# Gate and up projections as seven-product 2x2 blocks with paused PSUM groups, and a steady stage laid out by time

## The chip, the cores and the metric

The kernel runs on one core of one Trainium2 chip. The metric is device time in microseconds, the median of several runs. The engines are TensorE (PE, matmuls; PEld are its weight loads), VectorE (DVE), ScalarE (ACT), GpSimd (POOL) and SyncE (SP, which here issues the DMAs). PSUM is the accumulator memory of TensorE, in banks of 128 x 512 FP32. Each engine works through its own instructions in the order in which the program lists them, and engines wait for each other by semaphores.

## The reference

Input x is [1, 2048, 576] in FP32. It is normalised; then an attention with 32 heads of 18 columns and a sliding window of 256 tokens is multiplied by the SiLU of a bilinear gated feed-forward layer with 4608 inner columns, and x is added.

```python
def _A_ref(x, wqkv, wo):
    H = 32; Dh = D // H; W = 256
    q, k, v = (x @ wqkv).reshape(B, S, 3, H, Dh) ...          # one per 576 columns
    scores = jnp.einsum("bhqd,bhkd->bhqk", q, k) * (Dh ** -0.5)
    mask = (idx[:, None] - idx[None, :] >= 0) & (idx[:, None] - idx[None, :] < W)
    p = _softmax(jnp.where(mask[None, None], scores, -1e9), axis=-1)
    return jnp.einsum("bhqk,bhkd->bhqd", p, v) ... @ wo

def _B_ref(x, w_gate, w_up, w_down):
    g = jnp.einsum("bsd,df->bsf", x, w_gate)
    u = jnp.einsum("bsd,df->bsf", x, w_up)
    return jnp.einsum("bsf,fd->bsd", g * u, w_down)

xn = _layernorm(x, axis=-1)
return x + _A_ref(xn, wqkv, wo) * _silu(_B_ref(xn, w_gate, w_up, w_down))
```

## The kernel before

Everything that TensorE multiplies is split into an FP16 high part and an FP16 low part, and a product is made as three passes (high x high, high x low, low x high). A product here means one matmul instruction: 128 contraction rows, 128 output rows, up to 512 columns, added up in a PSUM bank. With 576 = 4.5 x 128 contraction rows, a gate or up tile of 128 inner rows x 512 tokens takes 13 full products (`full_passes`, L896) and a half-height one of 64 rows (`half_pass`, L899 and L900, gate and up side by side as a pair).

*Prologue, to 184 us.* x is loaded, normalised and transposed into `XT` (high and low parts, tokens as columns); `XT2` holds the last 64 rows a second time, for the half products. V, Q and K are computed in two halves of 1024 tokens (`qk_tile`: L323 the products, L327 ACT's copy out, L328 DVE's low part) and stored to DRAM.

*Steady stage, 72 slots.* A slot is one of 18 groups of 256 inner rows and one of four chunks of 512 tokens. In a slot PE makes two gate tiles and two up tiles. ACT copies the gate tile out of PSUM (`gate_out`, L742, tile `gt`), DVE multiplies the up tile with it (`up_out`, L747, `ht`), and h is split (`h_hi` L752 on ACT, `h_lo` L757 on DVE). One slot later `down` makes 8 groups of six 288-column products (L770) in the single PSUM bank `dn`; DVE adds each to `acc` straight behind it (L775, the eviction).

One attention step (two heads, 512 queries) also runs in each of 64 slots. PE makes four scores at a time (L647); DVE adds the mask and takes the maximum (L655, `mx`); POOL makes of that the bias of the exponential (L657); ACT takes the exponential (L662, `sm_`) and casts it to the high part (L665, `pp`); the low part is a subtraction on DVE for one head and on POOL for the other (L670); SP issues the transpose by DMA (L673, `pt`); PE multiplies with V (L682, bank `pv`, `weigh`), and `finish` divides by the sum. Step s runs in slot s + 1.

The weights of the next group are prepared beside this. `ffn_raw` loads gate, up and down weights into `raw0`, `raw1`, `raw2`; `ffn_amax` (L356) takes maxima over their rows on DVE; `ffn_spread_out` joins them, two tiles in one (`am`), and writes them to DRAM (`sd_f`, L132); `ffn_spread_in` reads them back to all partitions (L136, `spread`); `ffn_scale` (L369 and the small operations L122 to L126) makes power-of-two scales `sc` of them on DVE; ACT (L147) and DVE (L150) split the weights with these, and POOL scales the high part of the down weights (L394).

*End, from about 1589 us.* The last down groups, then 16 `o_out`: the output projection (L860), SiLU, product, sum and store, with loads (`o_load`) four token tiles ahead.

*What sets the order.* Nothing reorders instructions. In the steady stage `at(slot, place, f, ...)` enters a step into one of 16 places of a slot, and the last loop walks through slots and places: at each place it lists 3 or 4 products, then the steps entered there, scores first and down groups next. That order is the order of every engine's queue and of SP's DMA issues.

```python
for n in range(8):
    at(sl + 1, (... (7, 9, 11, 13, 15, 17, 19, 21))[n], down, sl, n)
```

A place beyond 15 falls into the next slot.

Of the kernel before, what the change touches and what calls it, by code (L numbers as in the profile page):

```python
# [20 lines left out]
def kernel(  # L21
# [66 lines left out]
    def up_ring():  # L88
        return ring.tile([128, 10, 128], F16, name="upw", bufs=8)

    def dn_ring():
        return ring.tile([128, 3, D], F16, name="dnw", bufs=4)

    def h_ring():
        return ring.tile([128, 2, 512], F16, name="hh", bufs=4)

    def f_ring(name):
        return ring.tile([128, 512], F32, name=name, bufs=1)
# [8 lines left out]
    idle = const.tile([128, 512], BF, name="idle")  # L107
# [12 lines left out]
    def power(m, p, s):  # L120

        nc.vector.tensor_scalar(p, m, LEAST, MOST, op0=OP.max, op1=OP.min)  # L122
        pi = p.bitcast(mybir.dt.int32)
        nc.vector.tensor_scalar(pi, pi, 0x7F800000, None, op0=OP.bitwise_and)
        nc.vector.reciprocal(s, p)
        nc.vector.tensor_scalar(s, s, WTOP, None, op0=OP.mult)  # L126
# [38 lines left out]
    def full_passes(w, c):  # L165
        return passes(w, XT[:, :, c * 512:(c + 1) * 512])

    def half_pass(w, c, upper):

        r = slice(64, 128) if upper else slice(0, 64)  # L170
        return w[r, 9], (XT2[r] if upper else XT[r, 4])[:, c * 512:(c + 1) * 512]

# [5 lines left out]
    XN = {}  # L178
# [6 lines left out]
    XR = {}  # L185
# [9 lines left out]
    def stats(t):  # L195
# [8 lines left out]
        XN[t] = (sm, q)  # L204
# [15 lines left out]
    def parts(a, eng, src, h):  # L220
        eng.tensor_tensor(a[:, D:D + 64], src[:, 512:D], h[:, 512:D], op=OP.subtract)
        eng.tensor_tensor(a[:, D + 64:2 * D], src[:, 0:512], h[:, 0:512], op=OP.subtract)

    def norm1(t):
        xr, (sm, q) = XR.pop(t), XN[t]
        xn = XN[t] = pro.tile([128, D], F32, name="xn", bufs=3)
        nc.scalar.activation(xn, xr, AF.Identity, bias=sm[:, 3, q:q + 1], scale=sm[:, 1, q:q + 1])

    def norm2(t, whole=True):
# [21 lines left out]
    def turned(t, a=None, b=None):  # L251
# [6 lines left out]
        nc.scalar.copy(XT2[64:128, cs], b[64:128])  # L258
        nc.scalar.copy(XT[0:64, 4, cs], b[0:64])

    def turned_low(t, eng=nc.vector):
# [3 lines left out]
        eng.tensor_tensor(XT[64:128, 4, cs], b[64:128], XT2[64:128, cs], op=OP.subtract)  # L265
# [6 lines left out]
    rqk = pro.tile([128, 5, 2 * D], F32, name="rqk")  # L272
# [94 lines left out]
    def ffn_scale(g):  # L367
        sc = SC[g] = ring.tile([128, 12], F32, name="sc", bufs=3)
        nc.vector.tensor_reduce(sc[:, 0:3], SC.pop((g, "sp")), axis=AX.X, op=OP.max)  # L369
        power(sc[:, 0:3], sc[:, 3:6], sc[:, 6:9])  # L370
        nc.gpsimd.tensor_tensor(sc[:, 9:10], sc[:, 3:4], sc[:, 4:5], op=OP.mult)
        nc.gpsimd.tensor_scalar(sc[:, 9:10], sc[:, 9:10], C_FFN, None, op0=OP.mult)
        nc.gpsimd.tensor_tensor(sc[:, 9:10], sc[:, 9:10], sc[:, 5:6], op=OP.mult)

    def up_hi(g, k):
        w = UW[g, k] = up_ring()
        hi(w[:, 0:5], RAW[g, k % 2][:, :, k // 2 * 128:k // 2 * 128 + 128], SC[g][:, 6 + k % 2:7 + k % 2])

    def up_lo(g, k):
        w = UW[g, k]  # L380
# [140 lines left out]
    for t in range(16):  # L521
# [24 lines left out]
        if t % 8 < 7:  # L546
            continue
# [392 lines left out]
```

## Time and profile before

| what | us |
| --- | --- |
| median of 3 runs | 1653.02 (1652.64 to 1653.95) |
| span of the profiled execution | 1651.6 |
| prologue, to the first slot | 183.7 |
| one slot, first quarter of them / the others | 19.36 / 19.83 |
| steady stage ends, about | 1589 |
| PE busy | 1638.3 (99%) |
| DVE / ACT / POOL busy | 1185.1 / 913.6 / 596.2 |

The span is that of one profiled execution; its own time is not recorded beside it, so the runs' median stands 1.4 us above the span. A row of the page's groups reads: line, engine, operation, output tile <- input tiles, shape, count | busy time, mean ns of one | idle time of the engine before it and who ended it. A row of the chain or timeline reads: start, length, engine, line, operation. In a row of stretches stand length, then busy time and count for PE, PEld, DVE, ACT and POOL, the granted clock of PE, the share of DMA time and GB/s. SPq is SP's queue with its DMA issues.

### The profile page before, as it was taken

Reading aid. Unit: us, or ns where it says so; the run is one execution under the profiler, and the core shown is the slowest. Engines: PE = TensorE matmul, PEld = TensorE weight load, DVE = VectorE, ACT = ScalarE, POOL = GpSimd, SP = SyncE. Lnnn points to the kernel's source line nnn. Section 1 sums busy time; section 2 is a strip of 40 time slices with the busy share of each in tenths; the row PEclk is TensorE's granted clock in tenths of the full one; section 3 lists DMA queues with packets and bytes.
Section 4 is the critical chain, followed back from the end, with each engine's and each line's share of the span. In section 5 each row is a group of like instructions: output and inputs, shape, how many; then the busy total and the mean of one; then the engine's idle time right before and its main releaser. Section 6 shows DMA issues by size and latency. Waiting matters only on the chain.

```text
span 1651.6 us, 33875 instructions
## 1 busy us (share of the span) xinstructions
PE 1638.3 (99%) x12307; PEld 933.2 (56%) x12307; DVE 1185.1 (72%) x2985; ACT 913.6 (55%) x1578; POOL 596.2 (36%) x1043
## 2 busy tenths in 40 slices
PE   8999999999999999999999999999999999999999
PEld 5464455555555555555555555555555555555577
DVE  7533577777777878787878777878787787865544
ACT  6431465656565666676666666665666666632230
POOL 3110134445343535454444444444444443511000
PEclk9999999999999999999999999999999999999999
DMA  9482445455556766665666575757665656650228
GB/s 239 134 216 90 116 84 115 90 114 104 114 106 132 142 124 135 109 146 112 145 135 142 105 147 105 151 105 145 138 135 113 140 116 129 126 123 28 60 69 219
DMA packets 535079, 206.39 MB, mean 125 GB/s; under 512 B 473856, under 2 KB 513664, under 8 KB 534912
## 3 DMA queue, kind: packets, MB, share of 16 engines
q1 hardware_dynamic: 534912, 204.23, 57.8%
q8 instruction: 97, 1.59, 0.4%
q14 instruction: 70, 0.57, 0.1%
HBM read 76.63 MB, written 23.75 MB: 61 GB/s over the span
## 4 chain that ended last, share of the span: by engine, by line
PE 93%; DMA 3%; DVE 1%; SPq 1%; POOL 1%; issue 1%; ACT 0%; POOLq 0%; ACTq 0%
PE up L896 47%; PE dn L770 25%; PE up L323 5%; PE pv L682 4%; PE up L899 3%; PE s L647 2%; DMA pt<-pp 2%; PE s L860 2%; PE up L860 1%; PE s L291 1%; PE s L770 1%; PE up L291 1%; SPq L337 1%; DMA xr<-in_A_x_dram 0%; SPq L238 0%
## 5 line engine op out<-in xcount | busy, mean ns | idle before, releaser
L896 PE MATMUL up<-XT,upw 128*128 128x512 f16 x3744 | 926.8, 378 | 0.0
L770 PE MATMUL dn<-dnw,hh 128*128 128x288 f16 x3360 | 504.5, 286 | 0.0
L896 PEld LDWEIGHTS <-upw 128*128 128x128 f16 x3744 | 331.1, 97 | 279.6 <-issue 0.6
L775 DVE SCALAR_TENSOR_TENSOR acc<-dn,sc,acc 128x288 f32<-128x288 f32 x528 | 272.2, 516 | 285.9 <-PE dn L770 285.8
L770 PEld LDWEIGHTS <-hh 128*128 128x128 f16 x3456 | 326.1, 98 | 199.0 <-issue 41.1
L657 POOL TENSOR_SCALAR mx<-mx,sig 128x1 f32<-128x1 f32 x512 | 193.5, 378 | 551.3 <-DVE mx L655 526.2
L682 PEld LDWEIGHTS <-pt 128*128 128x128 f16 x2880 | 137.3, 96 | 62.9 <-DMA pt<-pp 5.2
L682 PE MATMUL pv<-vt,pt 128*128 128x37 f16 x2880 | 143.0, 179 | 2.9 <-DMA pt<-pp 2.9
L742 ACT ACTIVATE gt<-up 128x512 f32<-128x512 f32 x144 | 85.4, 593 | 84.5 <-PE up L899 81.4
L752 ACT ACTIVATE hh<-ht 128x512 f16<-128x512 f32 x144 | 89.9, 624 | 61.5 <-DVE ht L747 61.5
L747 DVE SCALAR_TENSOR_TENSOR ht<-up,gt 128x512 f32<-128x512 f32 x144 | 99.0, 688 | 16.6 <-PE up L896 6.6
L757 DVE SCALAR_TENSOR_TENSOR hh<-hh,ht 128x512 f16<-128x512 f16 x144 | 98.7, 685 | 0.0
L323 PE MATMUL up<-XT,upw 128*128 128x512 f16 x448 | 97.0, 379 | 0.0
L356 DVE TENSOR_REDUCE am<-raw 128x1 f32<-128x640 f32 (+1 forms) x108 | 85.0, 787 | 3.0 <-DMA raw<-in_B_w_gate_dram 3.0
L394 POOL TENSOR_SCALAR dnw<-dnw 128x576 f16<-128x576 f16 x36 | 69.1, 1921 | 23.0 <-ACT dnw L147 20.3
L147 ACT ACTIVATE upw<-raw,sc 128x640 f16<-128x640 f32 x72 | 59.2, 824 | 26.1 <-DVE sc L126 26.1
L323 PEld LDWEIGHTS <-upw 128*128 128x128 f16 x448 | 43.8, 98 | 52.5
L328 DVE SCALAR_TENSOR_TENSOR qp<-up,qp 128x512 f16<-128x512 f32 x36 | 24.7, 685 | 59.4 <-ACT qp L327 42.7
L150 DVE SCALAR_TENSOR_TENSOR upw<-raw,sc,upw 128x640 f16<-128x640 f32 x72 | 63.1, 876 | 0.1
L647 PE MATMUL s<-ks,qs 54*128 54x384 f16 (+2 forms) x512 | 60.2, 312 | 0.0
L327 ACT ACTIVATE qp<-up 128x512 f16<-128x512 f32 x36 | 21.4, 597 | 66.6 <-PE up L323 56.1
L899 PE MATMUL up<-XT,upw 64*128 64x512 f16 x144 | 55.7, 387 | 0.0
(2227 smaller groups left out, 2123.1 us busy)
## 6 DMA issues: line engine op xcount, KB each, us to landing
raw<-in_B_w_down_dram SPq DMA_DIRECT2D x36, 288.0 KB
raw<-in_B_w_gate_dram SPq DMA_DIRECT2D x36, 256.0 KB
raw<-in_B_w_up_dram SPq DMA_DIRECT2D x36, 256.0 KB
qk_d<-qp SPq DMA_DIRECT2D x112, 72.0 KB
vt<-v_d SPq DMA_DIRECT2D x48, 111.0 KB
ks<-qk_d SPq DMA_DIRECT2D x96, 54.0 KB
v_d<-vo SPq DMA_DIRECT2D x16, 296.0 KB
xr<-in_A_x_dram SPq DMA_DIRECT2D x16, 288.0 KB
```

What stands on the lines that cost most here:

```text
L323: nc.tensor.matmul(ps, a, b, start=i == 0, stop=i == len(pl) - 1)
L647: nc.tensor.matmul(ps[:, :hi_ - lo_], QS[s][r, i * 128:(i + 1) * 128], KS[s][r, lo_:hi_], start=True, stop=True)
L657: nc.gpsimd.tensor_scalar(mx[:, 1:2], mx[:, 0:1], sig[:, 1:2], shift, op0=OP.mult, op1=OP.add)
L682: nc.tensor.matmul(PVB[s][:, j, i, :VW], pt[:, 2 * nb * j + n], VT[s][:, lo_ + n % nb, j * VW:(j + 1) * VW], start=n == 0, stop=n == 2 * n ...
L742: nc.scalar.activation(g, ps, AF.Copy, scale=G_SC)
L747: nc.vector.scalar_tensor_tensor(h, ps, U_SC, GT.pop((sl, ft)), op0=OP.mult, op1=OP.mult)
L752: nc.scalar.activation(hh[:, 0], h, AF.Copy, scale=1.0 / LO)
L757: nc.vector.scalar_tensor_tensor(hh[:, 1], hh[:, 0], -LO, h, op0=OP.mult, op1=OP.add)
L770: nc.tensor.matmul(ps[:, :HALF], a, b, start=q == 0, stop=q == len(l) - 1)
L775: nc.vector.scalar_tensor_tensor(d, ps[:, :HALF], SC[g][:, 9:10], d, op0=OP.mult, op1=OP.add)
L896: nc.tensor.matmul(banks[up], a, b, start=i == 0 and not up, stop=i == 12 and up == 1)
L899: nc.tensor.matmul(banks[0], *half_pass(w, c, False), start=False, stop=True)
```

## The change

*Gate and up as blocks.* The unit of work becomes 128 gate rows and the same 128 up rows by 1024 tokens, taken as two sets of four 128-token tiles (even and odd). The contraction is cut into two halves of two 128-row blocks. The 2x2 block product is then formed from seven products P1 to P7 of sums of weights (`ws`, made on POOL by `ffn_sums` from `raw0` and the rescaled `raw1`) and sums of tokens (`TX`, made once from the transposed x by `t_form`; `t1` takes the place of x's odd tiles in `XT`). Each is six matmuls. The last 64 rows are made without blocks: `t11`, `t22` with two matmuls, `t21`, `t12` with one and a half-height one. A slot is group, tile k of the two, half q of the tokens, so there are 72 again.

*Paused groups.* Bank A collects P1, P6, P7, P4 and a tail; bank C collects P2, P5 and P3 with tails. Both are read in the middle of their accumulation: A by ACT after P1, P6 and P7 (`copy_out`), C by DVE after P2, P5 and P3 (`add_out`). `times_0` on DVE multiplies from A at the end, `times_1` on POOL multiplies what lies in SBUF.

*Order by time.* `at(slot, t, ...)` now takes a time within a slot of 18.65, `W` holds most of the times, and all steps are sorted by it. Down groups run three slots later and two groups behind that, so that 26 of them follow the last slot. Maxima, spread and scale stand closer to each other.

*Attention.* The score's operation on DVE multiplies by a scale and takes a minimum, a small ACT copy makes the bias, POOL's step L657 goes; exponentials stay single; the casts on ACT and the subtractions, now all on POOL, take both heads at once. Buffers of `pp` go from 3 to 2, of `pt` from 3 to 4. Scores are made in one slot ahead (0 and 1) and in the slot itself (2 and 3). Outputs of attention are stored every fourth step.

*Elsewhere.* `XT2` and its copies go. At the end `o_load` runs eight tiles ahead, into buffers of the weights.

```diff
+    def t_form(p, step):
+        q, m = divmod(p, 4)
+        cs = slice(2 * p * 128, (2 * p + 2) * 128)
+        t1 = t1s[:, m]
+        to = TX[:, q, :, :, m * 128:(m + 1) * 128]
+        if step == 0:
+            nc.gpsimd.tensor_tensor(x32p, XT[:, 0:4, cs], XT[:, 5:9, cs], op=OP.add)
+        elif step == 1:
...
+            for d, a, b in ((t1, o1, e1), (tf[:, 0], o2, t1), (tf[:, 1], o2, o1), (tf[:, 2], e2, tf[:, 0])):
+                nc.vector.tensor_tensor(d, a, b, op=OP.subtract)
+        elif step == 2:
+            nc.scalar.copy(to[:, :, 0:2], tf)
+            nc.vector.tensor_tensor(to[:, :, 2:4], tf, to[:, :, 0:2], op=OP.subtract)
...
+    def ffn_ratio(g, k):
+        r = RAW[g, 1][:, :, k * 128:(k + 1) * 128]
+        nc.gpsimd.tensor_scalar(r, r, SC[g][:, 10:11], 1.0 / WF, op0=OP.mult, op1=OP.mult)
+    def ffn_sums(g, k, part):
...
+            nc.gpsimd.tensor_tensor(s_[:, d:d + 2] if d < 8 else s_[:, 8], x_, y_, op=op)
...
-        nc.gpsimd.tensor_scalar(mx[:, 1:2], mx[:, 0:1], sig[:, 1:2], shift, op0=OP.mult, op1=OP.add)
...
-        nc.scalar.activation(sm, sm, AF.Exp, bias=mx[:, 1:2], scale=sig[:, 0:1])
...
+        nc.vector.tensor_tensor_reduce(sm[:, j, :n], ps[:, :n], bias[:, 384 - n:], sig[:, 1:2], 3e38,
+                                       op0=OP.add, op1=OP.min, accum_out=mx[:, j:j + 1])
+    def probs(s, i):
+        nc.scalar.activation(mx[:, 2:4], mx[:, 0:2], AF.Copy, bias=shift)
+        for j in range(2):
+            nc.scalar.activation(sm[:, j, :n], sm[:, j, :n], AF.Exp, bias=mx[:, 2 + j:3 + j], scale=-1.0)
+    def probs_hi(s, i):
+        nc.scalar.copy(pp_of(s, i)[:, :, 0], sm[:, :, :n])
...
-        (nc.gpsimd if j else nc.vector).tensor_tensor(pp[:, a + n:a + 2 * n], sm, pp[:, a:a + n], op=OP.subtract)
...
+        nc.gpsimd.tensor_tensor(pp[:, :, 1], sm[:, :, :n], pp[:, :, 0], op=OP.subtract)
...
-        todo.setdefault(slot * 16 + place, []).append((f, a))
+    T = 18.65
+    W = {"ttr": [0.18, 0.51, 3.42, 3.58, ...], ..., "amax": [13.45, 14.1, 14.89, 14.7, 17.23, 17.23], "scale": 7.11, ...}
+    def at(slot, t, f, *a):
+        todo.append((slot * T + t, len(todo), f, a))
...
+    PROD = {"P1": (0, 0, 5, "e1"), "P2": (0, 2, 5, "e2"), "P3": (2, 6, 9, "o2"), "P4": (1, 0, 3, "t4"),
+            "P5": (2, 0, 9, "t1"), "P6": (2, 2, 9, "t2"), "P7": (2, 4, 9, "t3")}
+    TAIL = {"t11": (0, 4, 5, 0), "t21": (1, 2, 3, 0), "t22": (1, 2, 3, 1), "t12": (2, 8, 9, 1)}
...
+    def copy_out(sl, name, bk):
+        FT[sl, name] = f_ring()
+        nc.scalar.activation(FT[sl, name], BK[bk], AF.Copy, scale=E_SC)
+    def add_out(sl, name, bk):
+        nc.vector.scalar_tensor_tensor(f, BK[bk], E_SC, f, op0=OP.mult, op1=OP.add)
+    def times_0(sl):
+        nc.vector.scalar_tensor_tensor(f, BK["A"], E_SC, f, op0=OP.mult, op1=OP.mult)
+    def times_1(sl):
+        nc.gpsimd.tensor_tensor(f, f, FT[sl, "a3"], op=OP.mult)
...
+            for kind, t in ((1, 0.0), (2, 0.3), (0, 11.5)):
...
+                    at(b - 3, t + 0.1 * part, ffn_raw, g, kind, part)
+            for n in range(6):
+                at(b - 3, W["amax"][n], ffn_amax, g, (1, 1, 2, 2, 0, 0)[n], n % 2)
+            at(b - 3, 18.2, ffn_spread_out, g)
+            at(b - 2, 2.0, ffn_spread_in, g)
+            at(b - 2, W["scale"], ffn_scale, g)
...
+    def down_at(sl, n, t):
+        u = 8 * (sl - 3) + n - LAG
+        if 0 <= u < NDOWN:
+            at(sl, t, down, u)
+            at(sl, t + 0.75, down_out, u)
+    for sl in range(NSLOT):
+        at(sl, 0.0, prod, sl, "A", "P1", 0, 6, True)
+        at(sl, 1.3, copy_out, sl, "a1", "A")
+        down_at(sl, 0, 1.29)
+        at(sl, 2.03, prod, sl, "C", "P2", 0, 4, True)
+        down_at(sl, 1, 2.9)
+        at(sl, 3.62, prod, sl, "C", "P2", 4, 6)
+        at(sl, 4.0, tail_, sl, "C", "t11")
+        at(sl, 4.49, add_out, sl, "a1", "C")
+        at(sl, 5.2, prod, sl, "A", "P6")
+        at(sl, 6.5, copy_out, sl, "a2", "A")
+        down_at(sl, 2, 6.5)
+        at(sl, 7.25, prod, sl, "C", "P5", 0, 4, True)
+        down_at(sl, 3, 8.5)
+        at(sl, 9.25, prod, sl, "A", "P7")
+        at(sl, 10.56, copy_out, sl, "a3", "A")
+        at(sl, 10.55, prod, sl, "C", "P5", 4, 6)
+        at(sl, 11.0, tail_, sl, "C", "t22")
+        at(sl, 11.45, add_out, sl, "a3", "C")
+        down_at(sl, 4, 11.4)
+        at(sl, 12.15, prod, sl, "A", "P4")
+        at(sl, 13.5, tail_, sl, "A", "t21", False)
+        down_at(sl, 5, 13.7)
+        at(sl, 14.45, prod, sl, "C", "P3", 0, 3)
+        down_at(sl, 6, 15.1)
+        at(sl, 15.85, prod, sl, "C", "P3", 3, 6)
+        at(sl, 16.5, tail_, sl, "C", "t12", False)
+        at(sl, 16.7, tail_half, sl, "A", "t21")
+        at(sl, 16.8, tail_half, sl, "C", "t12")
+        at(sl, 17.0, times_0, sl)
+        at(sl, 17.6, add_out, sl, "a2", "C")
+        down_at(sl, 7, 17.9)
...
```

DVE in the slot in which the maxima of a group are taken, after the change. L880 is `times_0`, L876 `add_out` (tiles `ft`), L372 the maxima, L377 their join, L920 the eviction of a down group:

```order
L880 SCALAR_TENSOR_TENSOR ft_9780<-up_9752,ft_9780 128x512
L372 TENSOR_REDUCE am_9964<-raw0_9944 128x1 x2
L876 SCALAR_TENSOR_TENSOR ft_9842<-up_9753,ft_9842 128x512
L377 TENSOR_TENSOR am_9964<-am_9964 128x3
L920 SCALAR_TENSOR_TENSOR acc_1962<-dn_10034,sc_7848,acc_1962 128x288
```

The maxima of the gate weights stand between the two last reads of PSUM in that slot, and the join ahead of the eviction of the eighth down group.

SP in the same place, after the change. L748 are the transposes of probabilities, L786 and L789 the stores of attention's output, L124 and L128 the way of the maxima out to DRAM and back:

```order
L748 DMA_TRANSPOSE pt_9962<-pp_9959 128x12x128
L786 DMA o_d1_84<-ob_9047 128x4x144
L789 DMA o_d1_84<-ob_9047 128x4x144
L124 DMA sd_f8_10042<-am_9964 128x3
L128 DMA spread_10072<-sd_f8_10042 128x384
L748 DMA_TRANSPOSE pt_10093<-pp_10086 128x12x128
```

SP before, in the corresponding place (L132 and L136 are the two ways, L673 the transposes, L634 the load of V):

```order
L132 DMA sd_f9_11759<-am_11318 128x3
L634 DMA vt_11775<-v_d_82 128x6x74
L673 DMA_TRANSPOSE pt_11820<-pp_11773 128x12x128
L711 DMA o_d1_84<-ob_7159 128x1152
L136 DMA spread_11849<-sd_f9_11759 128x384
L673 DMA_TRANSPOSE pt_11896<-pp_11823 128x12x128
```

The way out and the way back had three other transfers between them and now follow each other.

DVE in the slot after that, before the change (L369 and L122 to L126 are the scale, L775 evictions, L655 the scores):

```order
L670 TENSOR_TENSOR pp_11967<-sm__11927,pp_11967 128x384
L775 SCALAR_TENSOR_TENSOR acc_1888<-dn_11976,sc_10764,acc_1888 128x288
L369 TENSOR_REDUCE sc_11990<-spread_11849 128x3
L122 TENSOR_SCALAR sc_11990<-sc_11990 128x3
L124 TENSOR_SCALAR sc_11990<-sc_11990 128x3
L125 RECIPROCAL sc_11990<-sc_11990 128x3
L126 TENSOR_SCALAR sc_11990<-sc_11990 128x3
L775 SCALAR_TENSOR_TENSOR acc_1888<-dn_12024,sc_10764,acc_1888 128x288
```

And DVE there after the change (L892 is `h_lo`, L385 and L114 to L118 the scale):

```order
L876 SCALAR_TENSOR_TENSOR ft_10067<-up_10046,ft_10067 128x512
L892 SCALAR_TENSOR_TENSOR hh_10099<-hh_10099,ft_9842 128x512
L385 TENSOR_REDUCE sc_10146<-spread_10072 128x3
L114 TENSOR_SCALAR sc_10146<-sc_10146 128x3
L116 TENSOR_SCALAR sc_10146<-sc_10146 128x3
L117 RECIPROCAL sc_10146<-sc_10146 128x3
L118 TENSOR_SCALAR sc_10146<-sc_10146 128x3
L920 SCALAR_TENSOR_TENSOR acc_1962<-dn_10131,sc_7848,acc_1962 128x288
```

In both the scale stands between two evictions; it has stands in the slot right behind the one whose maxima it reads.

ACT in the slot in which most of a tile's weights are split, after the change (L139 are the high parts of weights, L872 `copy_out`, L729 the small copy, L731 exponentials, L736 the cast):

```order
L139 ACTIVATE wg_9256<-raw0_8795,sc_8997 128x640
L872 ACTIVATE ft_9266<-up_9179 128x512
L139 ACTIVATE wu_9340<-raw1_8599,sc_8997 128x384
L729 ACTIVATE mx_9289<-mx_9289 128x2
L731 ACTIVATE sm__9288<-sm__9288,mx_9289 128x384 x2
L139 ACTIVATE ws_9347<-sums_9126,sc_8997 128x512
L872 ACTIVATE ft_9351<-up_9179 128x512
```

Three splits of weights now stand around two copies out of PSUM bank A, where before the splits stood between exponentials and casts and one copy out per half slot.

523 lines of the change are left out of this document (299 added, 224 removed).

## The prediction

> **What bounds it now.** I read the page's engine shares and chain first, then who TensorE waits for, then a piece of the chain inside the steady stage, then the busy times of single slots.
>
> ```profile
> span 1651.6 us, 33875 instructions
> PE 1638.3 (99%) x12307; PEld 933.2 (56%) x12307; DVE 1185.1 (72%) x2985; ACT 913.6 (55%) x1578; POOL 596.2 (36%) x1043
> PE 93%; DMA 3%; DVE 1%; SPq 1%; POOL 1%; issue 1%; ACT 0%; POOLq 0%; ACTq 0%
> ...
> PE pv L682 <- DMA pt<-pp: 2.9, 5, 0.9
> ...
> 847.53 0.73 PE dn L770 x6
> 848.27 1.29 PE up L896 x6
> ...
> 850.30 0.14 PE pv L682 x6
> ...
> 851.46 0.65 PE up L896 x3
> ...
> 854.14 0.32 PE up L899
> 854.46 0.00 PE up L900
> 854.46 0.33 PE s L647 x4
> 854.79 0.84 PE dn L770 x6
> ...
> 923.56:943.40 19.84, 19.84 (x163) 11.25 (x163) 15.41 (x42) 11.77 (x20) 9.33 (x17) 1.00 0.52 111
> 943.40:963.20 19.80, 19.80 (x161) 11.22 (x160) 16.16 (x41) 14.46 (x26) 9.59 (x15) 1.00 0.63 117
> ```
>
> TensorE is busy for 99% and makes 93% of the chain; all its waits for other engines together are a few us. In the pieces of the chain (start, length, what) a 512-column product costs 1.29/6 = 0.215, a group of six down products 0.73 (0.84 just after scores), a pair of half-height products 0.32 (0.10 of it before the first starts), four scores 0.33, six PV products 0.14. The last two rows are one slot each: length, then busy time of PE, PEld, DVE, ACT, POOL. A slot takes 19.8 with no hole in PE at clock 1.00; DVE has about 4 us to spare, ACT 5 to 8, POOL 10. So time falls as fast as products are taken from PE, until a handoff to another engine shows.
>
> **What goes.** Before, a slot holds 4 x 13 = 52 full gate/up products and two half pairs. After: seven products of six, six full ones for the last 64 rows, and one half pair: 48 full and one pair. Per slot 4 x 0.215 = 0.86, and of a pair 0.22; its other 0.10 I leave in, since the scores at 7.02 then follow full-height products directly. 1.08 x 72 slots = **-77.8 us**. Added up by the same rows, the new slot lasts 18.7: P1 1.29, then down groups, products and attention in the order of the table, with the seventh down group ending at 18.7.
>
> **What is added beside it.** For the costs I take these rows.
>
> ```profile
> L775 DVE SCALAR_TENSOR_TENSOR acc<-dn,sc,acc 128x288 f32<-128x288 f32 x528 | 272.2, 516 | 285.9 <-PE dn L770 285.8
> L747 DVE SCALAR_TENSOR_TENSOR ht<-up,gt 128x512 f32<-128x512 f32 x144 | 99.0, 688 | 16.6 <-PE up L896 6.6 <-ACT pp L665 2.8 <-issue 0.9
> L742 ACT ACTIVATE gt<-up 128x512 f32<-128x512 f32 x144 | 85.4, 593 | 84.5 <-PE up L899 81.4 <-PE s L647 1.8
> L147 ACT ACTIVATE upw<-raw,sc 128x640 f16<-128x640 f32 x72 | 59.2, 824 | 26.1 <-DVE sc L126 26.1
> L356 DVE TENSOR_REDUCE am<-raw 128x1 f32<-128x640 f32 x72 | 58.2, 809 | 3.0 <-DMA raw<-in_B_w_gate_dram 3.0
> L208 ACT ACTIVATE sm<-mv,eps_t 128x2 f32<-128x2 f32 x8 | 2.4, 296 | 11.2 <-DVE mv L203 11.2
> ...
> 909.99 0.71 ACT L662 ACTIVATE sm__12853<-sm__12853,mx,sig 128x384 f32<-128x384 f32 x1 [0.29 <-POOL mx L657]
> 910.73 0.51 ACT L665 CAST pp<-sm__12853 128x384 f16<-128x384 f32 x1
> ...
> 910.03 0.91 POOL L670 TENSOR_TENSOR pp<-sm__12824,pp 128x384 f16<-128x384 f32 x1
> ...
> L670 POOL TENSOR_TENSOR pp<-sm__8300,pp x1: 1603/1603/1603, 620.0 to 620.0; 128x384 f16<-128x384 f32 x1
> ```
>
> DVE per slot: two more PSUM reads (2 x 0.69) and some 450 more weight columns (0.6), less four subtractions (of the size that takes POOL 0.91) that go to POOL: about even, 15 to 16 of 18.7. ACT: one more copy out (0.59), four small copies (4 x 0.30), 0.6 of weights, less what four wide casts save against eight: 13 to 15. POOL: four double subtractions of at most 2 x 0.92 (7.4), one product, sums and ratio, less eight bias steps: 12 to 14. No engine reaches 18.7, so what the edits cost is waits at single handoffs. Four of these I price.
>
> (a) *Down groups six and seven.* The single `dn` bank goes to DVE and back.
>
> ```profile
> 901.61 0.90 PE L770 MATMUL dn<-dnw,hh 128*128 128x288 f16 x6
> 902.54 0.52 DVE L775 SCALAR_TENSOR_TENSOR acc<-dn,sc,acc 128x288 f32<-128x288 f32 x1 [1.09 <-PE dn L770]
> ...
> 95.04 0.69 DVE L328 SCALAR_TENSOR_TENSOR qp<-up,qp 128x512 f16<-128x512 f32 x1 [5.39 <-DMA qk_d<-qp]
> 95.79 1.46 PE L323 MATMUL up<-XT,wq 128*128 128x512 f16 x6 [1.45 <-DVE qp L328]
> ```
>
> PE is free for its next product at 901.61 + 0.73 = 902.34, DVE starts 0.20 later and takes 0.52; PE starts 0.06 after DVE's end. A round trip is 0.78 even with DVE idle. Between `down_at(sl, 5, ...)` and `down_at(sl, 6, ...)` stand three products, 0.65: a wait of 0.13 in each of the 69 slots with down groups, **+9.0**. Every other gap has four products (0.86) or more. Behind the waiting group stands everything on PE, so it is paid in full.
>
> (b) *The maxima slot* (one of four). DVE holds, after the last products of bank A: `times_0` 0.69, two maxima 0.81 each, `add_out` 0.69, the join of the maxima 0.16, then the eviction 0.52. From 18.7 - 1.8 + 0.13 + 0.20 = 17.3 that ends at 21.0. The next slot's first down group wants the bank at 18.85 + 1.29 = 20.14. That would be 0.9; neighbours on DVE may overlap in part, which can bring it to nothing. I take the middle, 0.4 x 16 = **+7**, between 0 and 0.9 each.
>
> (c) *The scale chain.* The maxima go to DRAM and come back to all partitions before DVE's `ffn_scale`, which stands ahead of an eviction in DVE's order.
>
> ```profile
> 1474.74 0.33 SPq L132 DMA_DIRECT2D sd_f<-am  x1
> ...
> 1477.05 0.32 SPq L136 DMA_DIRECT2D spread<-sd_f  x1
> ...
> 1531.75 0.33 SPq L132 DMA_DIRECT2D sd_wo<-woa  x1
> 1539.24 0.33 SPq L136 DMA_DIRECT2D spread<-sd_wo  x1
> ...
> 921.04 0.83 SPq L132 DMA_DIRECT2D sd_f<-am  x1
> ...
> 926.38 0.53 SPq L136 DMA_DIRECT2D spread<-sd_f  x1
> ...
> 169.95 0.35 SPq L136 DMA_DIRECT2D spread<-sd_f  x1
> 173.80 0.67 DVE L369 TENSOR_REDUCE sc<-spread 128x3 f32<-128x384 f32 x1 [0.71 <-DMA spread<-sd_f]
> 175.12 0.17 DVE L126 TENSOR_SCALAR sc<-sc 128x3 f32<-128x3 f32 x1
> ```
>
> The way out takes 2.3 (1474.74 to 1477.05) up to 7.5 (the `wo` pair), in the steady stage at most 5.3 (921.04 to 926.38); the way back 3.85 (169.95 to 173.80); the scale itself 1.5. Before, these stood some 16 us apart. After, the maxima are joined at about 20.1 of their slot, the two transfers follow each other on SP, and `ffn_scale` is reached by DVE at about 5.9 of the next slot. I take 2.5 out, near the row that has an `o_d` store beside it as here: 20.2 + 2.5 + 0.1 + 3.85 = 26.65, or 7.8 of the next slot. Scale until 9.3, eviction and release until 9.9; PE wants the bank for its fourth down group at 8.5, with (b) at 8.9. Stall about 0.9 x 16 = **+14**; with 2.3 out 0.7, with 5.3 out 3.7. Queued behind it on DVE: two scores, `finish`; on POOL the ratio; on SP nothing, since the way out has landed by then.
>
> (d) *The weights slot* (one of four). On ACT, between the first and the third copy out, stand 0.59 + 3 small copies 0.9 + 6 exponentials 4.3 + two casts of at most 2 x 0.9 + one 0.62 + weights 0.82, 0.6 and 0.72 + two copies 1.2 = 11.5, from 1.5: it ends at 13.0, or 12 with overlaps, where the fourth product wants bank A at 12.1. 0.25 x 17 = **+4**, between 0 and 0.9.
>
> At the start, slots 0 to 2 have no down groups: 12.8 us of PE each, against about 13 of ACT and chains of score, exponential, subtraction and transpose (0.33 + 0.7 + 0.9 + 4 or more). I put **+5** there, between 0 and 12.
>
> **At nothing.** The token sums in the prologue and the end's loads:
>
> ```profile
> 101.00:184.00 83.00, 83.00 (x483) 47.12 (x482) 27.43 (x49) 21.65 (x42) 3.49 (x8) 1.00 0.44 129
> 1596.00:1648.00 52.00, 51.95 (x425) 41.26 (x422) 25.62 (x47) 0.98 (x2) 0.00 (x0) 1.00 0.78 206
> ```
>
> From 101 to 184 DVE has 55 of 83 us free and POOL 79, while eight token pairs cost DVE under 3 each; if that cover went, at most the two copies before slot 0 (1.2) would show. At the end PE is full, so deeper loads can win nothing. The postponed down groups (26 x 0.73 = 19) only move. The 1.5 that PE waited at 95.79 may go with the dropped copies of x on SP, or stay.
>
> **Sum.** 1651.6 - 77.8 + 9.0 + 7 + 14 + 4 + 5 = 1612.8; the median of the runs (1653.0) lies 1.4 above the profiled span, so **1614**.
>
> [...]
>
> **Rivals.**
> *The waits hide* (chance 0.30): the maxima arrive before DVE, since neither (b), (c) nor (d) was ever seen as a PE wait. Then 1651.6 - 77.8 + 9 + 2 + 1.4 = 1586. For it: DVE has 3 us free per slot. Against: order on DVE, not load, makes (b) and (c).
> *The chain to DRAM is long* (0.10): each us more in (c) costs 16. The gain of 40 is gone when it takes 2.5 us more than taken, so 5.0 out; at the `wo` row's 7.5 it is 1614 + 80 = 1694. For it, the 5.3 bound and 7.5; against, that SP waits for this landing hardly ever.
> *ACT or POOL becomes the bound* (0.08): if POOL's subtractions all run at 1.6 per 384 columns, as the row at 620.0 did against 0.91 in most, POOL holds 12.8 + 6 = 19 a slot, and probabilities come late: 1635 to 1650.
> *Moving operands in pieces are slower* (0.04): 32 products a slot now read x in four runs of 128. A PV product of 37 columns takes 0.14/6 = 0.023, where 37/512 x 0.215 is 0.016; at 0.008 for each of three breaks that is 0.77 a slot, +55: 1669.
> *The clock* (0.03): PE idles briefly several times a slot. At half clock a slot would last 18.7 longer; four such slots undo the gain of 78. The rows above stand at 1.00. [...]
>
> **Chances.** The forecast's own case, parts of (a) to (d) paid, has 0.45 and spans 1598 to 1632. Range 1580 (all hidden but half of (a)) to 1648 (chain 2 us longer). No change is 0.2%, 3.3 us, about what can be told apart. Slower takes 0.07 of the long chain and ACT cases, the pieces' 0.03 and the clock's 0.01: 0.11; same 0.03; faster 0.86.
>
> **What would show it.** Full gate/up products 3744 before and 72 x 48 = 3456 after, 0.215 apart, slots of about 18.9; PE waits named `dn` <- DVE of 0.1 in every slot, larger every fourth, with DVE waiting for `spread`; `up` <- ACT small. Wrong if `dn` waits are absent, or if the slot lasts over 19.8.

## The result and the profile after

The changed kernel takes 1707.6 us (median of 4 runs, 1706.2 to 1709.1) against 1652.8 for the kernel before. The ratio is 1.032, 95% interval 1.031 to 1.034: slower, where 1614 was forecast. The profiled execution spans 1705.9, 54.3 more than before.

The page's engine shares and its chain that ended last, of the changed kernel:

```profile
PE 1602.6 (94%) x11875; PEld 907.6 (53%) x11875; DVE 1328.7 (78%) x2989; ACT 929.6 (54%) x1742; POOL 791.2 (46%) x823
...
PE 54%; DVE 18%; DMA 10%; SPq 3%; issue 1%; POOL 0%; ACT 0%; DVEq 0%; ACTq 0%
```

Its cores, with the mean granted clock of TensorE:

```profile
core 0: 1705.9 us, clock 0.984
```

Four rows of its waits (who waited for whom: total us, times, longest):

```profile
PE dn L908 <- DVE acc L920: 70.4, 48, 7.6
...
DVE sc L385 <- DMA spread<-sd_f: 29.9, 17, 3.2
DVE am L372 <- DMA raw<-in_B_w_gate_dram: 24.6, 13, 3.2
...
PE up L844 <- ACT ft L872: 11.2, 3, 4.1
```

PE's share of the chain fell from 93% to 54%, its clock is no longer 1.00, and it now waits for the eviction of `dn`. Behind the evictions stand two landings: `spread`, and the gate weights `raw0`. Each group of weights has four slots, called 4g to 4g+3 here; those of one group of the changed kernel (rows of stretches as before) show where:

```profile
1064.10:1083.00 18.90, 18.90 (x157) 10.76 (x155) 17.72 (x39) 13.45 (x26) 13.33 (x13) 1.00 0.55 95
1083.00:1102.10 19.10, 19.04 (x157) 10.76 (x155) 17.67 (x40) 12.29 (x23) 9.77 (x8) 1.00 0.73 179
1102.10:1126.90 24.80, 20.87 (x157) 11.25 (x155) 16.96 (x43) 11.16 (x21) 11.65 (x14) 0.93 0.75 130
1126.90:1145.80 18.90, 18.90 (x156) 10.73 (x154) 17.61 (x38) 13.55 (x26) 10.98 (x11) 1.00 0.56 97
```

Three of the four slots last 18.9 to 19.1, a little under a us less than the 19.8 of before. The third, 4g+2, lasts 24.8 (its median over the groups is 23.75) and eats more than the others save. The two waits of PE below lie in it. Inside it, rows of SP, DVE and PE in the timeline:

```profile
1094.52 1.91 SPq L694 DMA_DIRECT2D qs<-qk_d  x4
1096.47 0.40 SPq L702 DMA_DIRECT2D vt<-v_d  x1
1096.98 0.58 SPq L134 DMA_DIRECT2D raw<-in_B_w_gate_dram  x1
...
1102.65 1.55 DVE L372 TENSOR_REDUCE am<-raw 128x1 f32<-128x640 f32 x2 [1.46 <-DMA raw<-in_B_w_gate_dram]
...
1104.78 0.51 DVE L920 SCALAR_TENSOR_TENSOR acc<-dn,sc,acc 128x288 f32<-128x288 f32 x1
1105.34 0.90 PE L908 MATMUL dn<-dnw,hh 128*128 128x288 f16 x6 [1.81 <-DVE acc L920]
```

Then pieces of its chain that ended last (start, length, what):

```profile
1105.62 2.85 DMA sd_f<-am
1108.49 4.38 DMA spread<-sd_f
1112.89 0.67 DVE sc L385
1114.37 0.43 DVE acc L920
1114.85 0.90 PE dn L908 x6
1115.74 3.80 PE up L844 x10
```

And the stretch in which these ten products run:

```profile
1116.00:1119.40 3.40, 3.40 (x10) 1.23 (x9) 2.18 (x8) 2.72 (x7) 0.94 (x4) 0.51 1.05 99
```

`raw0` is free for its load at about 1093, when DVE's last split from it ends, but SP first issues a transpose and the loads of Q and V; the load starts at 1097, lands at 1102.65, and the maxima wait for it. So the eviction ahead of the slot's first down group ends late (first wait, 1.81). The way out and back then takes 2.85 + 4.38, the scale 1.5, and the fourth down group, at 1114.85, waits for the eviction behind it (second wait, 2.12 in the timeline). And then ten products take 3.80, where ten take 2.16 in the other slots: the granted clock is 0.51 for 3.4 us. Such stretches are called half clock below.

Added up over PE's rows, the waits and the time lost to half clock (share lost x length of each stretch) are, beside the forecast's terms:

| place | forecast | waits | half clock |
| --- | --- | --- | --- |
| slots 4g+2: (b) and (c) | 7 + 14 | 58.1 | 15.4 |
| slots 4g and 4g+1: (d) | 4 | 5.7 | 0 |
| (a), short gap, 0.13 in each of 69 slots | 9.0 | 9.0 | 0 |
| slots 0 to 2 | 5 | 14.4 | 6.8 |
| slot 69 (output weights' scale) | not named | 8.5 | 3.4 |
| prologue, later start of slot 0 | 0 | 6.3 in all | |

With the -77.8 of the products that gives +49.8, near the +54.3 of the spans; 4.5 stay unassigned.

### The profile page after: what moved, and what is told of

It reads as the page before. It is cut to its first block, busy times and chain, and to the rows that moved or that the text cites. A ratio compares the mean times of both kernels' runs of the same rounds, so it can differ in the third digit from the quotient of the medians.

```text
span 1705.9 us, 32395 instructions
## 1 busy us (share of the span) xinstructions
PE 1602.6 (94%) x11875; PEld 907.6 (53%) x11875; DVE 1328.7 (78%) x2989; ACT 929.6 (54%) x1742; POOL 791.2 (46%) x823
## 3 DMA queue, kind: packets, MB, share of 16 engines
q8 instruction: 93, 1.52, 0.4%
HBM read 76.63 MB, written 23.75 MB: 59 GB/s over the span
## 4 chain that ended last, share of the span: by engine, by line
PE 54%; DVE 18%; DMA 10%; SPq 3%; issue 1%; POOL 0%; ACT 0%; DVEq 0%; ACTq 0%
PE up L844 29%; PE dn L908 17%; DMA spread<-sd_f 4%; DVE ws L142 3%; DVE acc L920 3%; PE pv L757 2%; DMA sd_f<-am 2%; DMA raw<-in_B_w_gate_dram 2%; DVE ft L876 2%; PE s L1012 2%; PE up L1012 1%; PE s L715 1%; DVE am L372 1%; DVE hh L892 1%; DVE dnw L142 1%; DVE ft L880 1%
## 5 line engine op out<-in xcount | busy, mean ns | idle before, releaser
L908 PE MATMUL dn<-dnw,hh 128*128 128x288 f16 x3312 | 501.0, 288 | 73.6 <-DVE acc L920 70.4
L920 DVE SCALAR_TENSOR_TENSOR acc<-dn,sc,acc 128x288 f32<-128x288 f32 x520 | 266.5, 512 | 109.0 <-PE dn L908 108.1
L844 PEld LDWEIGHTS <-ws 128*128 128x128 f16 x1872 | 180.0, 99 | 192.4 <-issue 39.8
L844 PE MATMUL up<-XT,ws 128*128 128x512 f16 x1008 | 277.4, 386 | 0.3 <-DVE ft L876 0.3
L844 PE MATMUL up<-XT,wg 128*128 128x512 f16 x1008 | 254.6, 382 | 3.2 <-DVE ft L876 1.8
L884 POOL TENSOR_TENSOR ft<-ft 128x512 f32<-128x512 f32 x72 | 109.5, 1521 | 284.9 <-DVE ft L876 139.0
L844 PE MATMUL up<-TX,ws 128*128 128x512 f16 x864 | 216.0, 387 | 7.1 <-ACT ft L872 7.1
L872 ACT ACTIVATE ft<-up 128x512 f32<-128x512 f32 x216 | 127.8, 592 | 170.9 <-PE up L844 165.8
L876 DVE SCALAR_TENSOR_TENSOR ft<-up,ft 128x512 f32<-128x512 f32 x216 | 147.8, 684 | 45.6 <-PE up L844 36.1
L892 DVE SCALAR_TENSOR_TENSOR hh<-hh,ft 128x512 f16<-128x512 f16 x144 | 136.1, 945 | 1.2 <-ACT hh L888 1.2
L729 ACT ACTIVATE mx<-mx 128x2 f32<-128x2 f32 x256 | 51.0, 199 | 133.3 <-DVE mx L724 133.1
L339 PE MATMUL up<-XT,wq 128*128 128x512 f16 x504 | 111.4, 383 | 5.2 <-DVE qp L344 5.2
L844 PE MATMUL up<-TX,wu 128*128 128x512 f16 x432 | 106.7, 384 | 4.1 <-ACT ft L872 4.1
L372 DVE TENSOR_REDUCE am<-raw 128x1 f32<-128x640 f32 (+1 forms) x108 | 80.8, 788 | 24.6 <-DMA raw<-in_B_w_gate_dram 24.6
```

Source lines behind the costliest of these rows:

```text
L339: nc.tensor.matmul(ps, a, b, start=i == 0, stop=i == len(pl) - 1)
L372: nc.vector.tensor_reduce(SC[g, "am"][:, half, kind:kind + 1], r, axis=AX.X if kind == 2 else AX.XY, op=OP.max, apply_absolute_value=True)
L844: nc.tensor.matmul(ps.rearrange("p (m n) -> p m n", n=128), w, b, start=start, stop=stop, skip_group_check=True)
L872: nc.scalar.activation(FT[sl, name], BK[bk], AF.Copy, scale=E_SC)
L876: nc.vector.scalar_tensor_tensor(f, BK[bk], E_SC, f, op0=OP.mult, op1=OP.add)
L884: nc.gpsimd.tensor_tensor(f, f, FT[sl, "a3"], op=OP.mult)
```

## The experiments

The theory after the result, called *handoffs*: each of these waits is its own loss, made by what stands ahead in a queue, half clock follows them, and removing them adds up. The rival, *load*: DVE, 17.7 of 18.9 us busy, is the limit, and a wait taken away comes back at the next eviction. All times are medians; "before" was run beside each (1653.5 to 1654.3).

**The scale alone moved.**

```diff
-"sum0": [7.91, 15.69, 20.69], ... "scale": 7.11
+"sum0": [14.2, 15.69, 20.69], ... "scale": 12.6
```

> The changed kernel with one step moved: the scale of the next group's weights is reached by DVE at 12.6 instead of 7.11 of its slot, so that it stands behind the evictions of down groups three and four; the products made of it on POOL move with it (7.91 to 14.2). Theory 'handoffs' (each wait of TensorE in every fourth slot is its own loss, and they add up): of the two waits in that slot the second one (the eviction behind the scale, 26 us over the kernel) goes and with it about 10 of half clock; the first (the eviction behind the maxima, about 30) stays. 1707.5 - 36 = 1672, between 1660 and 1685. Rival 'load' (DVE, busy 16.5 of 18.9 us and slowed by POOL, is the limit, so that a wait taken away comes back at the next eviction): 1695 or more.

1664.1 (ratio to before 1.006, 1.004 to 1.008). The slot 4g+2 of the same group:

```profile
1076.40:1097.10 20.70, 19.09 (x157) 10.79 (x156) 17.12 (x43) 11.16 (x21) 10.96 (x13) 1.00 0.72 141
```

The second wait is gone and did not return; the first (1.6 here) stays. That is 43 us less, by a step moved within its slot: inside the range of *handoffs*, 8 below its middle.

**The whole chain moved.**

```diff
-"sum0": [7.91, 15.69, 20.69], ... "amax": [..., 17.23, 17.23], "scale": 7.11
+"sum0": [15.6, 16.2, 20.69], ... "amax": [..., 20.8, 20.8], "scale": 14.5
...
-            at(b - 3, 18.2, ffn_spread_out, g)
-            at(b - 2, 2.0, ffn_spread_in, g)
+            at(b - 2, 3.3, ffn_spread_out, g)
+            at(b - 2, 5.0, ffn_spread_in, g)
```

> The whole chain moved: the gate weights' maxima behind the first eviction of the next slot (20.8 instead of 17.23), the way out to DRAM at 3.3 and back at 5.0 of that slot, the scale at 14.5, what is made of it from 15.6. Theory 'handoffs': both waits of every fourth slot and their half clock go, 58 + 15 us less what the first groups keep; 1707.5 - 70 = 1637, between 1628 and 1648; the slot lasts 19 instead of 23.8. Rival 'load': the slot stays over 21 and the time over 1665.

1657.8 (1.0025, 1.0016 to 1.0035), 21 above the forecast and between the bounds of the two theories (1648 and 1665). Both old waits are gone, but in twelve groups a new one of 1.9 stands at the slot's third down group, and the timeline of DVE and POOL shows why. The stretch of one such slot:

```profile
1070.80:1091.70 20.90, 18.98 (x156) 10.71 (x154) 17.53 (x42) 11.10 (x21) 10.08 (x11) 1.00 0.83 144
```

POOL and DVE in it, by the timeline:

```profile
1075.12 1.98 POOL L745 TENSOR_TENSOR pp<-sm__14646,pp 128x768 f16<-128x768 f32 x1 [3.26 <-ACT pp L736]
...
1075.51 1.60 DVE L377 TENSOR_TENSOR am<-am 128x3 f32<-128x3 f32 x1
...
1078.11 0.51 DVE L920 SCALAR_TENSOR_TENSOR acc<-dn,sc,acc 128x288 f32<-128x288 f32 x1
```

The join of the maxima, three columns wide and 0.15 long in the changed kernel (1104.71, ahead of the eviction above), takes 1.60 here and ends with POOL's subtraction (1075.12 + 1.98 = 1077.10). So do the joins of all twelve groups; the six that find POOL idle take 0.15 to 0.16.

**The join by an operation with one input**, with the chain moved as before.

```diff
-        nc.vector.tensor_tensor(am[:, 0], am[:, 0], am[:, 1], op=OP.max)
...
+        nc.vector.tensor_reduce(am[:, 2], am[:, 0:2].rearrange("p h k -> p k h"), axis=AX.X, op=OP.max)
...
```

> The kernel with the chain moved, and the join of the maxima made by a reduction over one input instead of an operation on two. In the run before, the join of six numbers took 1.60 us on DVE while POOL ran a subtraction, and TensorE waited 1.9 us at the third down group of twelve slots. Theory 'lock' (a DVE operation with two inputs in SBUF waits until POOL's running operation ends): the reduction takes under 0.2, the 1.9 goes; 1658 - 23 = 1635, between 1628 and 1643. Rival 'order' (DVE simply has too much ahead of that eviction): the wait stays over 1.2 and the time over 1648.

1645.4 (0.994, 0.993 to 0.996), 12 less than the run before, 10 above the forecast. The line of the join (18 of it, shortest/median/longest in ns):

```profile
L377 DVE TENSOR_REDUCE am<-am x18: 151/153/161, 157.5 to 1453.1; 128x3 f32<-128x6 f32 x18
```

The slot 4g+2 of the same group:

```profile
1063.00:1082.50 19.50, 19.03 (x157) 10.76 (x155) 16.15 (x42) 10.88 (x21) 9.85 (x11) 1.00 0.82 151
```

In the same place, with the same subtraction of POOL under way, all twelve now take 0.151 to 0.156. So in this place it is the operation with two inputs in SBUF that waited, 1.60 against 0.15. The wait of PE at the third down group fell from 1.9 to 0.5 or less, not to nothing: part of *load* is right, since other operations with two inputs wait for POOL in its place (`h_lo` has a mean of 0.989 here, 0.945 in the changed kernel and 0.685 before the change).

**Four products in the short gap**, on top of that.

```diff
-        at(sl, 14.45, prod, sl, "C", "P3", 0, 3)
+        at(sl, 14.45, prod, sl, "C", "P3", 0, 4)
...
-        at(sl, 15.85, prod, sl, "C", "P3", 3, 6)
+        at(sl, 15.85, prod, sl, "C", "P3", 4, 6)
```

> The same with four instead of three products of P3 between down groups five and six. By term (a) of the prediction each of 69 slots loses 0.13 there, 9 us: 9 under the time of the kernel with the reduction (about 1626 if that is 1635). Rival: the 0.13 comes back at a later down group, within 3 of it.

1639.1 (0.991, 0.989 to 0.992): 6.3 less where 9 was expected. Slots 4g+3 went from 19.05 to 18.76 (medians), 4g from 19.07 to 19.17: where DVE is late anyway, the 0.13 comes back.

**TensorE kept busy with zeros**, all waits left in place.

```diff
+    zero = late.tile([128, 128], F16, name="zero")
+    nc.vector.memset(zero, 0.0)
...
+    def fill(sl, bk):
+        for _ in range(7):
+            mm(BK[bk], zero, xt(0, sl % 2, 0))
...
+        if sl % 4 == 2 and 16 <= sl < NSLOT - 4:
+            at(sl, 1.28, fill, sl, "A")
+            at(sl, 8.45, fill, sl, "C")
```

> Nothing is moved, but in every fourth slot from the fifth group on TensorE multiplies by zeros during its two waits (seven products of 0.215 ahead of the first and of the fourth down group, added to the open bank, so 1.5 us in each wait of 1.5 to 3.5). If half clock follows TensorE's own idle time, the clock stays at 1.00 in these slots and 10 to 15 us of 15 are saved, less 3 in the two slots that wait only once: 1692 to 1700. If half clock has another cause (power or the work of the chip), nothing is saved and up to 5 lost: 1707 to 1713.

1700.5 (1.028, 1.027 to 1.030), 7 less than the changed kernel although PE does 182 products more; that is 0.5 above the range of the first reading and well below that of the second. Its cores:

```profile
core 0: 1697.7 us, clock 0.992
```

In the profiled run none of the half clock is left in the slots 4g+2 (15.4 in the changed kernel); the 13.7 that remain lie in the prologue, the first slots and slot 69, where nothing was filled. So here half clock followed PE's own idle time: with the two waits filled the mean clock is 0.992, in the changed kernel 0.984.

**The gate weights loaded from another queue**, and entered 1.55 earlier.

```diff
-            raw_load(r, (w_gate, w_up)[kind], g * 256, 256, part)
+            raw_load(r, (w_gate, w_up)[kind], g * 256, 256, part, nc.scalar if g and kind == 0 else nc.sync)
...
-            for kind, t in ((1, 0.0), (2, 0.3), (0, 11.5)):
+            for kind, t in ((1, 0.0), (2, 0.3), (0, 9.95)):
```

> The changed kernel; only the loads of the gate weights are issued on ACT's DMA queue, entered at 9.95 instead of 11.5 of SP's, so that they don't stand behind a transpose and the loads of Q and V on SP. Theory 'late load' (the maxima wait for the gate weights to land, at 19.5 of their slot, and with them the first eviction of the next slot and the whole chain): the weights land some 4 us earlier, the first wait falls from 2.2 to under 0.9, the second by about 1, and most of the half clock goes: 13 x 1.5 + 13 x 1 + 12 = 44 less, 1664, between 1648 and 1682. Rival 'DVE order' (maxima, sum, join and eviction in a row are too long, whenever the weights land): the first wait stays over 1.5, 1690 or more.

1761.2 (1.065, 1.063 to 1.067): 97 above the forecast. The part that was asked came out: the first wait of the slots 4g+2 is 0.3, and they last 20.9 instead of 23.75, so the maxima were late because of the load. But PE now waits for ACT (waits of this kernel):

```profile
PE up L844 <- ACT ft L872: 72.2, 18, 5.9
```

ACT in one slot 4g+1, by the timeline:

```profile
615.70 0.37 ACTq L134 DMA_DIRECT2D raw<-in_B_w_gate_dram  x1
...
621.61 0.37 ACTq L134 DMA_DIRECT2D raw<-in_B_w_gate_dram  x1
...
622.56 0.60 ACT L872 ACTIVATE ft<-up 128x512 f32<-128x512 f32 x1 [4.46 <-DMA pt<-pp]
```

The second part of the load stood on ACT until a transpose of probabilities, issued by SP, had landed, and the copy out of bank A stood behind it. So here a DMA in an engine's queue made the engine wait, 4.46 us, for what the DMA waited for. Slots 4g+1 last 26.4 at the median, 19.1 in the changed kernel, with 6.83 us at half clock in twelve of the eighteen.

**The output weights' scale a slot later.**

```diff
-        at(NSLOT - 2, 3.5 * k, wo_split, k)
+        at(NSLOT - 2, 4.0 + 3.5 * k, wo_split, k)
...
-    at(b + 1, 14.0, wo_scale)
+    at(b + 2, 2.6, wo_scale)
```

> The scale of the output weights moved by one slot (from 14.0 of slot 69 to 2.6 of slot 70) and the split of these weights from 0 to 4.0 of slot 70. 'Handoffs': slot 69 loses its wait of 7.6 us and two windows of half clock (3.4): 1707.5 - 11 = 1696.5, between 1693 and 1700. 'Load': the evictions of slot 70 wait instead, 1702 to 1708.

1690.5 (1.023, 1.020 to 1.025), 17 less than the changed kernel, 6 below the forecast. In the chain of the changed kernel the two ways of these maxima were:

```profile
1570.74 8.21 DMA sd_wo<-woa
1578.96 5.71 DMA spread<-sd_wo
```

Slot 69 went from 27.5 to 18.0, so 9.5 of the 17 are this step's. In the profiled runs the rest is half clock elsewhere: 17.1 lost here against 23.9 there. Which of the other waits it follows differs between the two, so these 7 can't be put down to the step.

**The prologue's buffers.**

```diff
-    qpool = pro_stack.enter_context(tc.tile_pool(name="qpool", bufs=1))
     pro = pro_stack.enter_context(tc.tile_pool(name="pro", bufs=1))
+    qpool = pro_stack.enter_context(tc.tile_pool(name="qpool", bufs=1))
...
-            QP[m] = qpool.tile([128, 2, S // 2], F16, name="qp", bufs=2)
+            QP[m] = qpool.tile([128, 2, S // 2], F16, name="qp", bufs=3)
```

> The changed kernel, steady stage untouched, with a third buffer for Q and K on their way to DRAM and with that pool laid behind the prologue's other one, so that the first copies out of slot 0 don't overlap memory that is still being stored. Theory 'handoffs': the waits of 2.2, 0.6 and 2.0 in the first half of Q and K, the 4.0 in slot 0, and two to three windows of half clock (1.7 each) go: 1707.5 - 12 = 1695, between 1691 and 1700. Rival: the token sums on DVE, ACT and POOL slow the prologue, 1703 to 1708.

1693.6 (1.024, 1.023 to 1.025), 14 less than the changed kernel, as forecast. The first products of slot 0 in the timeline of the changed kernel:

```profile
189.99 3.46 PE L844 MATMUL up<-XT,wg 128*128 128x512 f16 x14
197.48 2.33 PE L844 MATMUL up<-TX,ws 128*128 128x512 f16 x6 [4.03 <-ACT ft L872]
```

And of this one:

```profile
182.10 3.46 PE L844 MATMUL up<-XT,wg 128*128 128x512 f16 x14
```

Slot 0 starts 1.6 before that of the kernel before (183.66), with all token sums still in the prologue: these cost nothing there. The 4.03 of slot 0 came from memory: the first copies out lay where Q and K were still being stored. But a wait of 3.48 for ACT, where the second weights' splits wait for POOL, shows in slot 0 instead, and slots 0 to 2 together last 57.3, as in the changed kernel. What is gained up to slot 3, 7.9, is gained in the prologue; the other 6 lie later, partly in fewer stretches of half clock.

**All of it**: the last chain, the four products, the output weights and the prologue's buffers, and the low parts of the down weights later.

```diff
-"dlo": 18.36
+"dlo": 20.8
```

> All of it together: the chain moved and joined by a reduction, four products in the short gap, the output weights' scale a slot later, the prologue's buffers, and the low parts of the down weights behind the next eviction (20.8 instead of 18.36). 'Handoffs': the gains add up, 1626 - 17 (output weights) - 11 (prologue) - 8 (the 0.2 to 0.6 in the two slots with weight splits) = 1590, between 1582 and 1602. 'Load': 1620 or more.

1617.6, ratio 0.978 (0.976 to 0.979): faster than the kernel before, but 28 above the forecast and between the bounds of the theories (1602 and 1620). The forecast started from 1626 for the run with four products, which came out at 1639. The four slots of the same group:

```profile
1011.90:1031.30 19.40, 18.84 (x156) 10.71 (x154) 18.41 (x39) 13.90 (x26) 13.29 (x13) 1.00 0.66 109
1031.30:1050.10 18.80, 18.80 (x157) 10.80 (x156) 17.69 (x41) 12.14 (x23) 9.52 (x9) 1.00 0.77 186
1050.10:1069.40 19.30, 18.83 (x156) 10.71 (x154) 15.96 (x42) 10.71 (x21) 9.67 (x11) 1.00 0.84 149
1069.40:1088.20 18.80, 18.80 (x157) 10.80 (x156) 17.96 (x39) 14.29 (x27) 13.79 (x14) 1.00 0.52 100
```

PE's largest wait in it:

```profile
PE dn L908 <- DVE acc L920: 16.7, 37, 1.0
```

PE's waits for the eviction fell from 70.4 to 16.7, the longest from 7.6 to 1.0. What is left of them, about 0.5 in slots 4g and 4g+2, did not add up as *handoffs* had it.

**Smaller steps between evictions.** One of the two maxima and the low parts behind the second eviction, with the way out behind them; one of POOL's subtractions and the load of the down weights later; and in slot 0 two splits of weights later.

```diff
-"plo": [3.42, ...], ... "dlo": 20.8, ... "amax": [..., 20.8, 20.8]
+"plo": [4.65, ...], ... "dlo": 22.4, ... "amax": [..., 20.8, 22.4]
...
-            for kind, t in ((1, 0.0), (2, 0.3), (0, 11.5)):
+            for kind, t in ((1, 0.0), (2, 5.0), (0, 11.5)):
...
-            at(b - 2, 3.3, ffn_spread_out, g)
+            at(b - 2, 4.6, ffn_spread_out, g)
...
+                    x_ = 2.5 if g == 0 and what in (1, 2) else 0.0
+                    at(c, W["whi"][what] + x_, w_hi, g, k, what)
+                    at(c, W["wlo"][what] + x_ / 2, w_lo, g, k, what)
```

> All changes of the version before, with smaller steps between evictions: one of the two maxima and the low parts of the down weights behind the second eviction of a slot (22.4 instead of 20.8), the way out at 4.6, the down weights loaded at 5.0 instead of 0.3, and in slot 0 the split of the second tile's weights behind the third copy out. Expected from the waits that were left (0.5 at the third down group in two slots of four, 3.5 and its half clock in slot 0): 1617.6 - 15 - 5 = 1598, between 1588 and 1608. Rival: DVE's waits for POOL move on to the next eviction, 1610 to 1620.

1653.8 (0.999, 0.998 to 1.000), 56 above the forecast: the gain is gone, by neither theory. The chain inside a slot 4g+2:

```profile
838.73 2.19 DMA sd_f<-am
840.94 5.44 DMA spread<-sd_f
846.40 0.30 SPq L694
...
847.11 2.61 DMA vt<-v_d
849.76 0.24 PE pv L757 x3
```

PE's new waits:

```profile
PE pv L757 <- DMA vt<-v_d: 11.1, 17, 1.1
PE s L715 <- DMA qs<-qk_d: 6.5, 10, 1.2
```

In this slot the way out is later, the last load of Q and the load of V come behind the landing of `spread` on SP's queue, and PE waits for them: 17.6 us in all for these two, 3.5 in the run before. The several steps were not tried one by one, so how much of the 36 us each has stays open; slots 4g+1 also grew, from 18.75 to 20.29.

## Why the prediction was wrong

The sum was 93 us too low (a span of 1705.9 against 1612.8). By the table, 52.5 of them lie at (b) and (c), 16.2 at the start, 11.9 at the output weights, 6.3 in the prologue and 1.7 at (d); 4.5 stay open.

**What goes: right.** A slot in which nothing else waits lasts 18.87, where the forecast's rows gave 18.7 + 0.13. The rival of moving operands in pieces falls too; P1 reads x in four runs and takes 0.215 a product (chain of the changed kernel):

```profile
1064.28 1.29 PE up L844 x6
...
1098.42 0.86 PE dn L908 x6
```

**(a): right.** The group behind the three products shows 0.86 instead of 0.73 (second row), the 0.13 of the forecast. Taking it away returned 6.3 of the 9, since part of it comes back at DVE.

**(b) and (c): the steps that failed, by size.** The place, the order on DVE and the two waits were right; 21 us became 73.5, of it 15.4 half clock. The prediction's own sign of being wrong, a slot over 19.8, came out in one slot of four. (Its 0.4 x 16 in (b) is 6.4 and not 7, which matters little.) In (b) the forecast put the maxima straight behind `times_0` and never asked when `raw0` lands: in the group shown its load starts 2.5 after the time in the table, behind other work on SP, and the maxima wait for it, over the kernel up to 3.2. With the load on another queue the first wait fell to 0.3. In (c) this passes on: the join ended 1.6 later than assumed, SP was 0.8 late with the way out, and the two ways took 2.85 + 4.38 instead of 2.5 + 3.85 (2.3 to 3.7 and 3.9 to 5.6 where they stand in the chain of the whole kernel). The sentence "on SP nothing" looked at what is queued behind the chain, but not at what is queued ahead of it.

**The clock: a rival at 0.03 that came true beside the others.** The forecast priced (b) to (d) at waits of 0.9 or less and half clock at nothing; in the group shown the waits were 1.81 and 2.12, and half clock stood behind the second. The 13 stretches of half clock in the changed kernel's records are each 3.41 us long or twice that, 54.6 us together, so half of it, 27.3 us, is lost. The starts of all 13 lie whole multiples of 3.413 apart. The length of a wait does not tell when: half clock came behind waits of 2.0 (at 87.73) and 2.1 (at 1114.85), while others of 2.8 (at 864.97) and 3.3 (at 1189.38) had none. What tells them apart in this kernel's records, from 20 us on, is PE's busy time in stretches of 3.413 counted from those starts: each of the 13 at full clock in which PE was busy for 1.42 us or less was followed by half clock, and none of the others, which have 1.52 or more (around the two waits without half clock 1.96 and 1.68 at the least). This is shown for this one profiled run; in that of `all_fixes2` the mean clock is 0.992, so some 13 of its 1653.1 us are lost, although at most five of PE's waits listed there are longer than 1.2.

**(d): right in size (5.7 for 4) by luck, wrong in place.** The wait lies on DVE, not on ACT (chain of the changed kernel):

```profile
1078.72 0.52 DVE acc L920
1079.24 1.63 DVE ws L142
```

Two of its groups by shape:

```profile
L142 DVE SCALAR_TENSOR_TENSOR ws<-sums,sc,ws 128x512 f16<-128x512 f32 x36 | 50.2, 1394 | 0.0
L892 DVE SCALAR_TENSOR_TENSOR hh<-hh,ft 128x512 f16<-128x512 f16 x144 | 136.1, 945 | 1.2 <-ACT hh L888 1.2
```

DVE's rows were costed as if POOL did not matter: a weight split of 512 columns has a mean of 1.39 (640 columns took 0.876 before), `h_lo` 0.945 instead of 0.685. Of the 144 `h_lo`, the 61 that found no operation of POOL with two inputs under way took 0.67 to 0.68; the other 83 took 0.72 to 1.71. Before the change none stood behind such an operation, and the longest took 0.69. An estimate from these durations, with and without POOL, for `h_lo`, the weight splits and `finish` gives 1.4 us a slot: most of why DVE is busy for 17.7 of a slot and not 15 to 16. The joins point the same way: 1.60 with two inputs beside a subtraction of POOL, 0.153 with one. So the edit counted as a relief, subtractions moved from DVE to POOL, came with longer operations on DVE; no run moves them back, so how much is due to them and how much to POOL's new sums and product stays open.

**The start: 21.2 for 5**, of it 4.03 and a length of half clock for memory that was still being stored; most of the rest lies in slots 1 and 2, where PE waits for ACT's copies out. With the memory moved the three slots were no shorter, since ACT's next wait took its place. **The prologue and the output weights, costed at nothing, cost 6.3 and 11.9.** For the output weights the forecast quoted the row of 7.5 as the upper bound for another chain and did not ask what waits for this one.

POOL did not become the bound (13.9 busy of 19.3 in its fullest slot), so that rival's step is refuted, though `h_lo` on DVE took up to 1.71 beside it.

The sign was wrong because the largest waits were priced with the length of their own chain and not with the queue ahead of it, and the half clock behind them with nothing. The case "the chain to DRAM is long", at 0.10, came nearest, but it reckoned with a way out of 5.0 and more: in the group shown the two ways took 0.9 longer than assumed, and the late start 2.4.

## What to carry to other kernels

Price a chain of transfers from when the issuing queue reaches it, with all that stands ahead there, and place what consumes it behind the evictions that TensorE needs. Where TensorE is the bound, count with the half clock that may follow its waits: in the changed kernel it came behind waits of 2.0 us and more, and cost 27.3 us. Before work is moved from DVE to POOL, look which DVE operations with two SBUF inputs will stand beside it (`h_lo` took up to 1.71 there and 0.67 to 0.68 alone), and give small joins one input (0.153 instead of 1.60).

## What the runs showed of the hardware that was not expected

A DVE operation on three columns took 1.60 us beside a POOL subtraction, in twelve cases of twelve, and 0.153 as an operation with one input in the same place. In the changed kernel TensorE's clock fell to half 13 times, for 3.41 us or twice that, each time behind 3.41 us in which PE had been busy for 1.42 us or less, also when no wait filled all of these, and stayed at 1.00 in the same slots when products with zeros filled 1.5 us of each wait. A load issued from ACT's queue held ACT for 4.5 us in the slot shown, until a transpose issued by SP had landed.
